# Attention with a soft mixture of experts on one core: all second layers as two column halves

## The chip, the core and the metric

The kernel runs on one core of one Trainium2 chip. The metric is the device time of one execution in microseconds, the median of several runs; lower is better. The engines are TensorE (PE, with its weight loads as PEld), VectorE (DVE), ScalarE (ACT), GpSimd (POOL) and SyncE (SP), which here issues all the DMAs.

## What is computed

First a causal attention with decay for 8 batches of 8 heads, 576 tokens and head size 64. Its result, reshaped to x of 4608 tokens by 512, goes through a soft mixture of 8 experts with 4 slots each:

```python
logits = x @ phi                                  # 4608 x 32
d = softmax of logits over the tokens             # how tokens make slots
slot_input = (d.T @ x).reshape(E, S_per_e, D)
for e in range(E):
    h = np.maximum(slot_input[e] @ w1[e], 0.0)    # 4 x 1024, "first layer"
    slot_out[e] = h @ w2[e]                       # 4 x 512,  "second layer"
c = softmax of logits over the slots              # how slots make tokens
return c @ slot_out.reshape(n_slots, D)           # 4608 x 512, float32
```

The output is 9.4 MB. The weights of the experts are 33.6 MB; the loads of the last 17 pieces of them are issued from 331.9 us on.

## The kernel before

The attention fills the first 324 us, head after head. The change touches only what comes behind it, the experts and the output; this part starts at about 331 us.

**Quarters.** The weights come in 64 pieces of 128 partitions by 1024 columns (512 KB), called quarters here. Eight belong to an expert: 0 to 3 are its first layer, 4 to 7 its second. `STEPS` (L34) is the order in which they are used, `ORDER` (L38) the order in which they are loaded; `weights(e, k)` finds one. 27 tiles hold the first ones, and when a step has used its quarters, `wstream` issues the next loads on SP into those tiles and into tiles of the attention that are free. SP issues in the order of the program.

**First layers.** `mlp1` makes the hidden values of an expert and `relu` gates them; `own` turns them so that `HT[e]` holds, for each of 8 chunks of 128 hidden units, a stationary matrix of 128x32.

**Second layers.** `mlp2(e, half, k)` multiplies one quarter with four matmuls of 256 columns each (in the trace each of them is two records, since float32 goes through TensorE in two passes). The stationary matrix has 32 columns, so four such matmuls write four different groups of 32 partitions of one PSUM bank. For experts below `DEFER` = 4, a quarter holds two chunks of hidden units over all 512 columns, and both halves of their steps add up in the bank `pv[0]`. For experts 4 to 7, a quarter holds four chunks over 256 columns, and columns 0 to 255 (half 0) add up in `po[0]`, columns 256 to 511 (half 1) in `po[1]`. The order is: experts 0 to 3 complete, half 0 of experts 4 to 7, half 1 of experts 4 to 7.

**From sums to output.** `so` takes the sum of experts 0 to 3 (ScalarE, L1002). When a half is complete, `gathered(n)` adds it (VectorE, L1012), `slots(n)` sums the four partition groups (TensorE, L1015), and `halve(n)` writes the result to `SO` as a rounded part (ScalarE, L1018) and the rest (VectorE, L1019). An output block is 128 tokens: `blocks(n0, n1, c)` multiplies the token weights with `SO`, 512 columns or one half of 256 (TensorE, L1032), copies each product out of PSUM, by turns on ScalarE and VectorE (L1033), into one of six staging tiles of 1024 columns, and issues a DMA for the call (SP, L1035). A half block of a token is a row of 1 KB in HBM, a full one 2 KB. A staging tile is used again when its DMA has landed.

**Token weights.** `cols(b)` turns the token weights of batch b for `blocks`, in four steps that `more(b, n)` takes: two transposes (L690), their cast (L694, ScalarE), three transposes, their casts (L694 and L696; VectorE for batches 2, 3, 5, 6, 7). Blocks of a batch can only go out behind its casts.

**The end.** While half 1 of experts 5 to 7 is multiplied, 10 half blocks of half 0 go out; three more stand between `gathered(1)` and `halve(1)`. Then follow half 1 of these 13 blocks and 23 full blocks. The order on every engine is the order of the program text.

Of the kernel before, what the change touches and what calls it, by code (L numbers as in the profile page):

```python
# [10 lines left out]
ALU = mybir.AluOpType  # L11
# [4 lines left out]
B, H, S, D = 8, 8, 576, 64  # L16
NE, SPE, DM, DF = 8, 4, 512, 1024
NS = NE * SPE
P = 128
# [9 lines left out]
NRES = 27  # L29
NQ = 8 * NE  # L30
QW = 1024
DEFER = 4

STEPS = tuple((e, 0) for e in range(8)) + tuple((e, k) for e in range(DEFER) for k in (4, 6)) + tuple((e, k) for k in (4, 6) for e in range(DEFER, 8))  # L34

SPLITS = {(6, 0): 4, (0, 6): 2, (1, 6): 3, (2, 6): 5, (3, 4): 6, (4, 4): 7}

ORDER = [8 * e + k + n for e, k in STEPS for n in range(2 if k else 4)]  # L38

# [29 lines left out]
def attn_softmoe(ctx: ExitStack, tc: tile.TileContext, qk, v, f, phi, w1, w2, cst, out):  # L69
    nc = tc.nc  # L70
# [51 lines left out]
    def wstream(*tiles):  # L122
        for t in tiles:
            axes = "abc"[: len(t.shape) - 1]
            t = t.rearrange(f"p {' '.join(axes)} -> p ({' '.join(axes)})")
            if len(quarter) < NQ:
                quarter.append(t[:, 0:QW])
                wload(len(quarter) - 1)

    def weights(e, k):  # L130
        return quarter[ORDER.index(8 * e + k)]
# [6 lines left out]
    pv = [psp.tile([P, 512], F32, name=f"pv{n}") for n in range(2)]  # L138
# [20 lines left out]
    def turn():  # L159
        ring.append(ring.pop(0))  # L160
        return ring[-1]
# [523 lines left out]
    def cols(b, bank):  # L685

        for ts in ((1, 2), (3, 4, 0)):
            pm = bank()
            for n, t in enumerate(ts):
                nc.tensor.transpose(pm[:, 128 * n : 128 * n + 128], CW[b][:, t].rearrange("p o r s -> p (o r s)").bitcast(F32), ident)  # L690
            yield
            at = S * b + 128 * (ts[0] - 1)
            copy = nc.vector.tensor_copy if b in (2, 3, 5, 6, 7) and 0 in ts else nc.scalar.copy
            copy(weights_of(at, 256).rearrange("p (u r c) -> p r u c", u=2, r=2), pm[:, 0:256].rearrange("p (r u c) -> p r u c", r=2, u=2))  # L694
            if 0 in ts:
                copy(weights_of(at + 256, 64), pm[:, 320:384])  # L696
            yield


    for g in range(1, NG):  # L700
        h0, h1 = 2 * g, 2 * g + 1
        u0, u1 = h0 + 3, h0 + 4
        b, w = divmod(g - 4, NPAIR)
# [154 lines left out]
    c = [cols(n, turn) for n in range(B)]  # L858
# [38 lines left out]
    po = [turn(), pv[0]]  # L897
    ring = [t for t in ring if t not in bank + po] + [st["lg", b]]
    HT = {}
# [8 lines left out]
    def mlp1(e, *ks):  # L908
        if e >= NE:
            return  # L910
        if 0 in ks:
            PH[e] = bank[e % 2]
        for k in ks:
            for j in range(4):
                nc.tensor.matmul(  # L915
                    PH[e][32 * j : 32 * j + 32, 0:256], slT[:, k, :], weights(e, k)[:, 256 * j : 256 * j + 256], start=(k == 0), stop=(k == 3)
                )

    def relu(e):

        scale = mk[:, e : e + 1]
        if e == 0:
            nc.vector.tensor_scalar(hs, PH[e][:, 0:256], scale, 0.0, op0=ALU.mult, op1=ALU.max)
        else:
            nc.vector.scalar_tensor_tensor(hs, in0=PH[e][:, 0:256], scalar=scale, in1=hs, op0=ALU.mult, op1=ALU.max)

    def blank_h(e):
        t = rest(e) if e < len(X) else quarter[NRES - 7 + e - len(X)][:, 640:896]
        HT[e] = t.rearrange("p (j c s) -> p j c s", j=4, c=2)
        nc.gpsimd.memset(HT[e], 0.0)  # L930

    def own():

        pm = turn()
        for c in range(2):
            nc.tensor.transpose(pm[:, 128 * c : 128 * c + 128], hs[:, 128 * c : 128 * c + 128], ident)
        for n in range(NE):
            mine = pm[:, 0:256].rearrange("p (c j s) -> p j c s", c=2, j=4)[:, :, :, 4 * n : 4 * n + 4]
            nc.vector.tensor_copy(HT[n][:, :, :, 4 * n : 4 * n + 4], mine)

    def mlp2(e, half, *ks):

        for k in ks or range(2):
            w = weights(e, 4 + 2 * half + k)
            for n in range(4 if e >= DEFER else 2):
                if e < DEFER:
                    fc, to = 4 * half + 2 * k + n, pv[0]
                    start, stop = e == half == 0, e == DEFER - 1 and half == 1
                else:
                    fc, to = 4 * k + n, po[half][:, 0:256]  # L950
                    start, stop = e == DEFER and k == 0, e == NE - 1 and k == 1
                m = to.shape[1]
                step = m if start or stop else 256
                for c in range(0, m, step):
                    nc.tensor.matmul(  # L955
                        to[32 * (fc % 4) : 32 * (fc % 4) + 32, c : c + step],
                        HT[e][:, fc // 2, fc % 2, :],
                        w[:, m * n + c : m * n + c + step],
                        start=start,
                        stop=stop,  # L960
                    )

    nc.vector.tensor_scalar_mul(mk, mk, fin[:, 2:3])
    for e in range(len(X)):
# [1 line left out]
    half = [slice(256 * n, 256 * n + 256) for n in range(2)]  # L966
    so = ctok.rearrange("p b t s -> p (b t s)")[:, 0:DM]
    used = 0
    for e, k in STEPS[:-4]:
        if k == 0:  # L970
            mlp1(e, 0, 1, 2, 3)
            relu(e)
        else:
            mlp2(e, k // 2 - 2)
        n = used + (2 if k else 4)
        wstream(*quarter[used : min(n, NRES)])
        used = n
        if (e, k) == (7, 0):
            next(c[4])
            next(c[4])  # L980
            own()
            next(c[4])
            next(c[4])
        if (e, k) == (1, 0):
            weigh(b)
            tokens(b, 0)
            combine(b, 0)
        if (e, k) == (3, 0):
            combine(b, 1)
            combine(b, 2)  # L990
        if (e, k) in SPLITS:
            split(SPLITS[e, k], 0, 1)
        if (e, k) == (6, 0):
            for n in range(len(X), NE):
                blank_h(n)
        if (e, k) == (0, 6):
            late.close()
            sp = ctx.enter_context(tc.tile_pool(name="sp", bufs=1))
            SO = sp.tile([P, DM], F32R, name="SO")
            last = [sp.tile([P, B // 2 * S - CUT[n]], F32R, name=f"cT{n}") for n in range(2)]  # L1000
        if (e, k) == (3, 6):
            nc.scalar.copy(so, pv[0])  # L1002

    pr = [t[:, 0:256] for t in bank]
    outv = out.rearrange("(n p) c -> p n c", p=P)
    NT = B * S // P
# [2 lines left out]

    def gathered(n):  # L1010

        nc.vector.tensor_tensor(so[:, half[n]], so[:, half[n]], po[n][:, 0:256], op=ALU.add)  # L1012

    def slots(n):
        nc.tensor.matmul(pr[n], srep, so[:, half[n]], start=True, stop=True)  # L1015
# [7 lines left out]
    def blocks(n0, n1, c=slice(0, DM)):  # L1023

        w = c.stop - c.start
        if state[1] + w * (n1 - n0) > QW:
            state[0:2] = state[0] + 1, 0
        o = stage[state[0] % len(stage)][:, state[1] : state[1] + w * (n1 - n0)]
        state[1] += w * (n1 - n0)
        for n in range(n0, n1):  # L1030
            pm = turn()[:, 0:w]
            nc.tensor.matmul(pm, weights_of(P * n, P), SO[:, c], start=True, stop=True)  # L1032
            copies[state[2] % 2](o[:, w * (n - n0) : w * (n - n0 + 1)], pm)  # L1033
            state[2] += 1
        nc.sync.dma_start(outv[:, n0:n1, c], o.rearrange("p (n c) -> p n c", c=w))  # L1035

    def more(b, n=2):

        for _ in range(n if b < B else 0):
            next(c[b])  # L1040

    gathered(0)
    mlp2(4, 1)
    slots(0)
    mlp2(5, 1)
    halve(0)
    ring += [po[0], bank[0]]
    blocks(0, 2, half[0])
    mlp2(6, 1)
    blocks(2, 4, half[0])  # L1050
    blocks(4, 6, half[0])
    mlp2(7, 1, 0)
    blocks(6, 8, half[0])
    blocks(8, 9, half[0])
    blocks(18, 19, half[0])
    mlp2(7, 1, 1)
    gathered(1)
    more(2, 1)
    blocks(19, 20, half[0])
    slots(1)  # L1060
    more(2, 1)
    blocks(20, 21, half[0])
    halve(1)
    blocks(21, 22, half[0])
    more(2, 1)
    ring += [po[1], bank[1]]
    then = {2: (2, 1), 4: (3, 2), 6: (3, 2), 18: (5, 2), 9: (5, 2), 13: (6, 2), 15: (6, 2), 22: (7, 2), 24: (7, 2)}
    for n0, n1 in ((0, 2), (2, 4), (4, 6), (6, 8), (8, 9), (18, 20), (20, 22)):
        blocks(n0, n1, half[1])
        more(*then.get(n0, (B,)))  # L1070
    for n0, n1 in ((9, 11), (11, 13), (13, 15), (15, 17), (17, 18)) + tuple((n, n + 2) for n in range(22, NT, 2)):
        blocks(n0, n1)
        more(*then.get(n0, (B,)))


# [39 lines left out]
```

## Time and profile before

| | us |
|---|---|
| median of 3 runs | 391.98 |
| lowest and highest run | 391.85 to 392.21 |
| span of the profiled execution, first to last instruction | 390.3 |
| TensorE busy in the span | 371.3 (95%) |
| VectorE busy | 280.4 (72%) |
| ScalarE busy | 259.6 (67%) |
| GpSimd busy | 252.5 (65%) |

Times inside the kernel are read from one profiled execution and count from its first instruction. The span lies 1.7 us below the median of the runs. Busy shares are means over stages that differ. The chain of waits follows the last instruction back to what released it. "DMA share" is the mean busy share of the core's 16 DMA engines in a stretch; when the queue is full it reads slightly over 1.

### The profile page before, as it was taken

Reading aid. Unit: us, or ns where it says so; the run is one execution under the profiler, and the core shown is the slowest. Engines: PE = TensorE matmul, PEld = TensorE weight load, DVE = VectorE, ACT = ScalarE, POOL = GpSimd, SP = SyncE. Lnnn points to the kernel's source line nnn. Section 1 sums busy time; section 2 is a strip of 40 time slices with the busy share of each in tenths; the row PEclk is TensorE's granted clock in tenths of the full one; section 3 lists DMA queues with packets and bytes.
Section 4 is the critical chain, followed back from the end, with each engine's and each line's share of the span. In section 5 each row is a group of like instructions: output and inputs, shape, how many; then the busy total and the mean of one; then the engine's idle time right before and its main releaser. Section 6 shows DMA issues by size and latency. Waiting matters only on the chain.

```text
span 390.3 us, 15100 instructions
## 1 busy us (share of the span) xinstructions
PE 371.3 (95%) x5867; PEld 333.4 (85%) x5867; DVE 280.4 (72%) x1074; ACT 259.6 (67%) x664; POOL 252.5 (65%) x349
## 2 busy tenths in 40 slices
PE   8989999999999999999999999999999998999860
PEld 8879999999999999999999999999999986567640
DVE  7968887878777978787878787878787635341670
ACT  8949776868686868677867786778776652021560
POOL 4977887878787878787878787878787841000000
PEclk9999999999999999999999999999999999999995
DMA  6874978676867787768677777777775889996798
GB/s 206 205 187 138 275 225 265 190 230 203 257 176 234 204 230 199 224 197 247 197 216 214 226 197 227 197 232 211 213 207 161 253 319 357 416 417 283 261 392 317
DMA packets 34343, 93.71 MB, mean 240 GB/s; under 512 B 4266, under 2 KB 8288, under 8 KB 34272
## 3 DMA queue, kind: packets, MB, share of 16 engines
q1 hardware_dynamic: 34272, 92.75, 76.4%
q8 instruction: 46, 0.75, 0.8%
q14 instruction: 25, 0.20, 0.1%
HBM read 63.93 MB, written 9.73 MB: 189 GB/s over the span
## 4 chain that ended last, share of the span: by engine, by line
PE 89%; DMA 5%; DVE 2%; ACT 1%; issue 1%; SPq 0%; ACTq 0%; DVEq 0%
PE pv L310 25%; PE ring L275 14%; PE s L222 12%; PE ring L276 12%; PE pv L337 4%; PE pv L955 4%; PE more L915 4%; PE lg L373 3%; PE ring L493 2%; DMA out<-RAW 2%; PE ds L457 2%; DMA V<-in_v 1%; PE pv L248 1%; DMA YA<-mr 1%; PE ring L1032 1%
## 5 line engine op out<-in xcount | busy, mean ns | idle before, releaser
L282 ACT ACTIVATE PTS<-ring 128x320 f32<-128x320 f32 (+2 forms) x256 | 119.5, 513 | 64.7 <-PE ring L276 39.7
L275 PE MATMUL ring<-YA,WA 67*128 67x320 f32 (+9 forms) x384 | 121.7, 330 | 0.1
L238 DVE CUSTOM_DVE_ANT_0 s<-s,mask 128x320 f32<-128x320 f32 (+3 forms) x256 | 109.1, 442 | 6.4 <-PE s L222 1.9
L276 PE MATMUL ring<-YB,WB 128*128 128x320 f32 (+4 forms) x384 | 110.6, 296 | 0.0
L310 PE MATMUL pv<-V,PTS 128*64 128x65 f32 x3200 | 104.5, 224 | 0.5 <-DMA V<-in_v 0.5
L310 PEld LDWEIGHTS pv<-V,PTS 128*64 128x64 f32 x3200 | 99.7, 138 | 3.3 <-issue 1.5
L222 PE MATMUL s<-WA,YA 66*128 66x288 f32 (+9 forms) x384 | 98.7, 313 | 0.9 <-ACT YA L180 0.8
L201 POOL TENSOR_TENSOR WB<-RAW,WB 64x576 fp32r<-64x576 f32 x64 | 90.5, 1414 | 12.4 <-DMA WB<-WA 7.2
L206 POOL TENSOR_TENSOR YB<-RAW,YA 64x576 fp32r<-64x576 f32 x64 | 89.7, 1419 | 2.5
L275 PEld LDWEIGHTS ring<-YA,WA 67*128 67x128 f32 (+3 forms) x384 | 69.9, 183 | 5.6 <-issue 2.1
L276 PEld LDWEIGHTS ring<-YB,WB 128*128 128x128 f32 (+1 forms) x384 | 70.1, 183 | 0.0
L222 PEld LDWEIGHTS s<-WA,YA 66*128 66x128 f32 (+1 forms) x384 | 63.1, 191 | 7.0 <-ACT PTS L282 1.3
L293 POOL TENSOR_SCALAR_AFFINE_SELECT PTS<-PTS 128x128 f32<-128x128 f32 (+1 forms) x128 | 31.3, 265 | 24.1 <-ACT PTS L282 22.2
L238 DVE DVE_READ_ACCUMULATOR2_ANT MT<- 128x1 f32 x310 | 44.0, 142 | 0.0
L290 POOL TENSOR_SCALAR_AFFINE_SELECT PTS<-PTS 128x384 f32<-128x384 f32 x64 | 33.3, 521 | 14.4 <-ACT PTS L282 10.4
L337 PE MATMUL pv<-cs,X 128*128 128x128 f32 x155 | 42.0, 277 | 0.0
L175 ACT CAST WA<-RAW 64x576 fp32r<-64x576 f32 x64 | 40.1, 669 | 1.2 <-DMA RAW<-in_qk 0.3
L180 ACT CAST YA<-RAW 64x576 fp32r<-64x576 f32 x63 | 39.5, 671 | 0.4
L238 DVE CUSTOM_DVE_ANT_0 s<-s,mask,MT 128x288 f32<-128x288 f32 x62 | 32.6, 526 | 9.0 <-PE s L222 0.2
L325 DVE TENSOR_SCALAR rl<-pv 128x5 f32<-128x5 f32 x64 | 10.5, 164 | 37.7 <-PE pv L310 37.1
L330 DVE TENSOR_TENSOR X<-pv,rl 128x320 f32<-128x320 f32 (+1 forms) x65 | 31.5, 486 | 2.4 <-DMA YA<-mr 0.3
L361 ACT COPY XTS<-pv 128x128 f32<-128x128 f32 (+1 forms) x124 | 28.6, 293 | 0.0
(214 smaller groups left out, 378.9 us busy)
## 6 DMA issues: line engine op xcount, KB each, us to landing
w<-in_w SPq DMA_DIRECT2D x45, 512.0 KB
RAW<-in_qk SPq DMA_DIRECT2D x31, 576.0 KB
V<-in_v SPq DMA_DIRECT2D x32, 325.0 KB
YB<-YA SPq DMA_DIRECT2D x30, 288.0 KB
WB<-WA SPq DMA_DIRECT2D x30, 288.0 KB
p<-in_w SPq DMA_DIRECT2D x6, 512.0 KB
out<-RAW SPq DMA_DIRECT2D x6, 512.0 KB
out<-p SPq DMA_DIRECT2D x5, 512.0 KB
```

The source lines that it names most:

```text
L175: nc.scalar.copy(WA[g % 3][0:64, S * h : S * h + S], RAW[g % 3][64:128, h])
L180: nc.scalar.copy(YA[g % 3][0:64, h, 64:640], RAW[g % 3][0:64, h])
L201: nc.gpsimd.tensor_tensor(t[0:64], RAW[g % 3][64:128, h], t[64:128].bitcast(F32), op=ALU.subtract)
L206: nc.gpsimd.tensor_tensor(YB[g % 2][64:128, h], RAW[g % 3][0:64, h], YA[g % 3][0:64, h, 64:640].bitcast(F32), op=ALU.subtract)
L222: nc.tensor.matmul(t[:, o : o + w], ya[0:m, h, 128 * blk : 128 * blk + 128], wa[0:m, j0 : j0 + w], start=True, stop=True)
L238: nc.vector.tensor_tensor_reduce(out=t[:, o : o + w], in0=t[:, o : o + w], in1=mask[:, m0 : m0 + w], scale=1.0, scalar=top if n == 3 else ...
L275: nc.tensor.matmul(o, wa[0:m, j0 : j0 + n], ya[0:m, h, 64 + i0 : 64 + i0 + w], start=True, stop=False)
L276: nc.tensor.matmul(o, wb[:, j0 : j0 + n], yb[:, h, i0 : i0 + w], start=False, stop=True)
L282: nc.scalar.activation(PT[i % 2][:, SEG_O[bank] : SEG_O[bank] + at], t[:, 0:at], AF.Exp, scale=0.125)
L290: nc.gpsimd.affine_select(d3, d3, pattern=[[0, 3], [1, 128]], compare_op=ALU.is_ge, fill=0.0, base=0, channel_multiplier=-1)
L310: nc.tensor.matmul(o[64 * u : 64 * u + 64, t, :], PT[i % 2][:, at : at + 64], V[:, g % 2, c, 65 * h : 65 * h + 65], start=(c == 0), stop=( ...
L337: nc.tensor.transpose(pm[:, 0:128], x[:, t, 128 * (p % 2) : 128 * (p % 2) + 128], ident)
```

## The change

All eight experts now use the 256-column layout that experts 4 to 7 had. The steps of the second layers become half 0 of experts 0 to 7, then half 1 of experts 0 to 7. `pv[0]` no longer holds a 512-wide sum, `so` takes no copy of it, and `gathered` becomes a copy. Host code lays the second-layer weights of experts 0 to 3 out like the others.

In the products of half 1, two quarters are followed by the slot sums of half 0, two more by the first two half blocks, and from there single quarters alternate with pairs of half blocks: 20 half blocks (10 pairs) stand between the products. Four more follow behind `halve(1)`. Transposes of token weights for batches 5, 2 and 3, which stood behind the products, now stand between them. Then come half 1 of the 24 blocks and 12 full blocks. So 48 half blocks and 12 full ones replace 26 and 23.

```diff
-DEFER = 4
-
-STEPS = tuple((e, 0) for e in range(8)) + tuple((e, k) for e in range(DEFER) for k in (4, 6)) + tuple((e, k) for k in (4, 6) for e in range(DEFER, 8))
-
-SPLITS = {(6, 0): 4, (0, 6): 2, (1, 6): 3, (2, 6): 5, (3, 4): 6, (4, 4): 7}
+STEPS = tuple((e, k) for k in (0, 4, 6) for e in range(8))
+
+SPLITS = {(6, 0): 4, (1, 4): 5, (2, 4): 2, (3, 4): 3, (4, 4): 6, (5, 4): 7}
...
-            for n in range(4 if e >= DEFER else 2):
...
+            for n in range(4):
+                nc.tensor.matmul(
+                    po[half][32 * n : 32 * n + 32, 0:256],
+                    HT[e][:, 2 * k + n // 2, n % 2, :],
+                    w[:, 256 * n : 256 * n + 256],
+                    start=e == k == 0,
+                    stop=e == NE - 1 and k == 1,
+                )
...
-    for e, k in STEPS[:-4]:
+    for e, k in STEPS[:-8]:
...
-        if (e, k) == (3, 6):
-            nc.scalar.copy(so, pv[0])
...
-        nc.vector.tensor_tensor(so[:, half[n]], so[:, half[n]], po[n][:, 0:256], op=ALU.add)
+        nc.vector.tensor_copy(so[:, half[n]], po[n][:, 0:256])
...
     gathered(0)
-    mlp2(4, 1)
+    mlp2(0, 1)
     slots(0)
-    mlp2(5, 1)
+    mlp2(1, 1)
     halve(0)
     ring += [po[0], bank[0]]
-    blocks(0, 2, half[0])
-    mlp2(6, 1)
-    blocks(2, 4, half[0])
-    blocks(4, 6, half[0])
-    mlp2(7, 1, 0)
-    blocks(6, 8, half[0])
-    blocks(8, 9, half[0])
-    blocks(18, 19, half[0])
-    mlp2(7, 1, 1)
+    early = [(0, 2), (2, 4), (4, 6), (6, 8), (18, 20), (20, 22), (22, 24), (24, 26), (8, 10), (10, 12)]
+    early_at = iter(early)
+    blocks(*next(early_at), half[0])
+    turns = {(3, 1): (5, 1), (4, 0): (5, 1), (4, 1): (5, 2), (5, 0): (2, 1), (5, 1): (2, 1), (6, 0): (2, 2), (7, 0): (3, 1)}
+    for e in range(2, NE):
+        for k in range(2):
+            mlp2(e, 1, k)
+            if (e, k) in turns:
+                more(*turns[e, k])
+            if (e, k) not in ((4, 1), (6, 0), (7, 1)):
+                blocks(*next(early_at), half[0])
     gathered(1)
-    more(2, 1)
-    blocks(19, 20, half[0])
+    more(3, 1)
     slots(1)
-    more(2, 1)
-    blocks(20, 21, half[0])
+    more(3, 2)
     halve(1)
-    blocks(21, 22, half[0])
-    more(2, 1)
+    early += [(12, 14), (14, 16)]
+    for n in early[-2:]:
+        blocks(*n, half[0])
     ring += [po[1], bank[1]]
-    then = {2: (2, 1), 4: (3, 2), 6: (3, 2), 18: (5, 2), 9: (5, 2), 13: (6, 2), 15: (6, 2), 22: (7, 2), 24: (7, 2)}
-    for n0, n1 in ((0, 2), (2, 4), (4, 6), (6, 8), (8, 9), (18, 20), (20, 22)):
+    then = {0: (6, 2), 4: (6, 2), 18: (7, 2), 22: (7, 2)}
+    for n0, n1 in early:
         blocks(n0, n1, half[1])
         more(*then.get(n0, (B,)))
-    for n0, n1 in ((9, 11), (11, 13), (13, 15), (15, 17), (17, 18)) + tuple((n, n + 2) for n in range(22, NT, 2)):
+    for n0, n1 in ((16, 18),) + tuple((n, n + 2) for n in range(26, NT, 2)):
         blocks(n0, n1)
-        more(*then.get(n0, (B,)))
...
-    w2 = np.concatenate([w2[:DEFER].transpose(0, 2, 1, 3, 4).reshape(DEFER, P, 8 * DM), w2[DEFER:].transpose(0, 2, 3, 1, 4).reshape(NE - DEFER, P, 8 * DM)])
+    w2 = w2.transpose(0, 2, 3, 1, 4).reshape(NE, P, 8 * DM)
```

The order on TensorE, at the end of the products of half 1 (in `L955 MATMUL pv_148<-w_121,w_132 32x256 x4`, the bank pv_148 takes the sums of half 1, w_121 is a quarter, w_132 holds an expert's `HT`). Before:

```order
L1015 MATMUL more_5693<-ctok,cs 128x256
L955 MATMUL pv_148<-w_123,w_133 32x256 x4
L955 MATMUL pv_148<-w_124,w_133 32x256 x4
L1032 MATMUL ring_152<-SO,cT 128x256
L1032 MATMUL ring_150<-SO,cT 128x256
L955 MATMUL pv_148<-w_125,w_134 32x256 x4
L955 MATMUL pv_148<-w_126,w_134 32x256 x4
L1032 MATMUL lg_5612<-SO,cT 128x256
L1032 MATMUL ring_151<-SO,cT 128x256
L1032 MATMUL pv_149<-SO,cT 128x256
L1032 MATMUL more_5693<-SO,cT 128x256
L955 MATMUL pv_148<-w_127,w_135 32x256 x4
```

After, from the same point behind half 0 (L1002 is the slot sum, L944 the product, L1019 the block):

```order
L1002 MATMUL more_5693<-ctok,cs 128x256
L944 MATMUL pv_148<-w_115,X_100 32x256 x4
L944 MATMUL pv_148<-w_116,X_100 32x256 x4
L1019 MATMUL ring_152<-SO,cT 128x256
L1019 MATMUL ring_150<-SO,cT 128x256
L944 MATMUL pv_148<-w_117,X_101 32x256 x4
L1019 MATMUL lg_5612<-SO,cT 128x256
L1019 MATMUL ring_151<-SO,cT 128x256
L944 MATMUL pv_148<-w_118,X_101 32x256 x4
L1019 MATMUL pv_149<-SO,cT 128x256
L1019 MATMUL more_5693<-SO,cT 128x256
L944 MATMUL pv_148<-w_119,X_5483 32x256 x4
```

The slot sum of half 0 moved ahead by eight quarters (w_115 follows it in place of w_123), and from w_117 on every quarter is followed by another kind of work.

The order on VectorE around the end of half 1 (L1012 gathers it, L1019 completes `SO`, L694 and L696 are casts of token weights, L1033 the copies of blocks). Before:

```order
L1033 COPY RAW_97<-ring_151 128x256
L1012 TENSOR_TENSOR ctok<-ctok,pv_148 128x256
L1033 COPY RAW_97<-ring_152 128x256
L1019 TENSOR_TENSOR SO<-more_5694,SO 64x256
L1033 COPY p_0_5327<-ring_151 128x256
```

After (L999 gathers, L1006 completes `SO`, L692 and L694 are the casts, L1020 the copies):

```order
L1020 COPY p_1_5328<-ring_152 128x256
L999 COPY ctok<-pv_148 128x256
L692 CAST cT_6017<-ring_150 128x2x2x64
L694 CAST cT_6017<-ring_150 128x64
L1006 TENSOR_TENSOR SO<-more_5694,SO 64x256
L1020 COPY p_0_5487<-ring_151 128x256
L1020 COPY p_0_5487<-more_5693 128x256
```

Two casts stand in the place of one copy ahead of the operation that completes `SO`, and the copies of the two fill pairs of half 0 stand behind it.

## Rows read from the trace of the kernel before

**Rows 1.** The page, chain that ended last: shares by engine.
```profile
PE 89%; DMA 5%; DVE 2%; ACT 1%; issue 1%; SPq 0%; ACTq 0%; DVEq 0%
```

**Rows 2.** Chain of waits from 300 us: start, duration, what.
```profile
347.11 11.49 PE pv L955 x192
...
372.73 8.62 DMA out<-RAW x2
```

**Rows 3.** Stretches of time: busy time by engine, granted clock, DMA share, GB/s.
```profile
348.00:357.00 9.00, 9.00 (x164) 7.42 (x163) 2.19 (x5) 1.98 (x5) 0.00 (x0) 1.00 1.02 416
357.00:358.00 1.00, 1.00 (x26) 0.93 (x21) 0.22 (x1) 0.00 (x0) 0.00 (x0) 1.00 0.76 299
358.00:361.00 3.00, 3.00 (x40) 1.42 (x36) 0.92 (x3) 0.74 (x2) 0.00 (x0) 1.00 0.07 30
361.00:362.00 1.00, 1.00 (x19) 0.53 (x8) 0.13 (x1) 0.00 (x0) 0.00 (x0) 1.00 0.08 16
362.00:364.00 2.00, 2.00 (x23) 0.98 (x22) 1.38 (x4) 1.29 (x4) 0.00 (x0) 1.00 0.46 157
364.00:367.00 3.00, 2.42 (x18) 1.85 (x15) 1.50 (x5) 1.29 (x4) 0.00 (x0) 1.00 1.09 379
367.00:369.00 2.00, 1.17 (x10) 0.96 (x10) 1.51 (x6) 1.04 (x4) 0.00 (x0) 1.00 0.71 238
369.00:373.00 4.00, 4.00 (x29) 3.47 (x27) 3.91 (x11) 3.76 (x10) 0.00 (x0) 1.00 1.03 345
373.00:388.00 15.00, 4.63 (x20) 2.65 (x18) 6.48 (x13) 4.94 (x10) 0.00 (x0) 0.72 1.05 399
388.00:390.30 2.30, 0.00 (x0) 0.00 (x0) 0.00 (x0) 0.00 (x0) 0.00 (x0) 0.50 0.17 65
```

**Rows 4.** TensorE in order of time: start, duration, line, operation, tiles, shapes, count.
```profile
354.03 4.57 PE L955 MATMUL pv<-w,w 128*32 128x256 f32 x80
358.53 0.70 PE L1015 MATMUL more<-ctok,cs 128*128 128x256 f32 x2
...
360.16 0.51 PE L1032 MATMUL ring<-SO,cT 128*128 128x256 f32 x2
360.60 1.07 PE L955 MATMUL pv<-w,w 128*32 128x256 f32 x16
...
362.26 0.64 PE L955 MATMUL pv<-w,w 128*32 128x256 f32 x8
362.83 0.51 PE L1032 MATMUL ring<-SO,cT 128*128 128x256 f32 x2
...
363.50 0.64 PE L955 MATMUL pv<-w,w 128*32 128x256 f32 x8
364.07 0.44 PE L690 MATMUL pv<-cs,w 128*128 128x128 f32 x2
...
364.69 0.70 PE L1015 MATMUL more<-ctok,cs 128*128 128x256 f32 x2
...
368.40 0.38 PE L690 MATMUL pv<-cs,w 128*128 128x128 f32 x2
...
368.86 0.49 PE L690 MATMUL pv<-cs,w 128*128 128x128 f32 x3
```

**Rows 5.** SyncE's queue: start, time and count of the output's first DMA issues.
```profile
361.23 5.19 SPq L1035 DMA_DIRECT2D out<-RAW  x8
```

**Rows 6.** VectorE in order of time, around the end of half 1.
```profile
360.71 0.42 DVE L1033 COPY RAW<-ring 128x256 f32<-128x256 f32 x1 [0.60 <-PE ring L1032]
...
364.21 0.42 DVE L1012 TENSOR_TENSOR ctok<-ctok,pv 128x256 f32<-128x256 f32 x1
...
366.00 0.43 DVE L1019 TENSOR_TENSOR SO<-more,SO 64x256 fp32r<-64x256 f32 x1
...
367.58 0.41 DVE L694 CAST cT<-lg 128x256 fp32r<-128x256 f32 x1
367.91 0.21 DVE L696 CAST cT<-lg 128x64 fp32r<-128x64 f32 x1
```

More of the change, by code (lines that the diff above doesn't have):

```diff
@@ L944, in mlp2 @@
             w = weights(e, 4 + 2 * half + k)
-            for n in range(4 if e >= DEFER else 2):
[L946 to L961, printed above, removed]
+            for n in range(4):
[6 more added lines that the diff above has]
+                )
     nc.vector.tensor_scalar_mul(mk, mk, fin[:, 2:3])
@@ L995, in attn_softmoe @@
                 blank_h(n)
-        if (e, k) == (0, 6):
+        if (e, k) == (1, 4):
             late.close()
```

## The prediction

> **What bounds the kernel now.** I read the shares of the chain of waits first. TensorE holds 89% of the chain and DMA 5% [rows 1], so a change in TensorE's order looks cheap or dear by TensorE's time alone. The end of the span says otherwise. The chain's last long piece is 8.62 us of output transfer, from 372.73 [rows 2], so I read the DMA share by stretches next [rows 3]. Four stages are to be seen there. Until 357 the queue is full with weights (share 1.02, 416 GB/s). About 357.8 the last weights land (0.76 of that one us) and the queue is all but empty until 362. From 362 to 369 it is fed in bursts (0.46, 1.09, 0.71). From 369 to 388.4 it is full without a break (1.03 and 1.05), while TensorE, VectorE and ScalarE fall idle. The reader should see two things: the end is set by when the output queue becomes full for good and by the bytes still due then, and before that point there is DMA time that nobody uses, some 6 us between 357.8 and 369 (1.93 MB went out there, 5.1 us of work at 379 GB/s, in 11.2 us). The change goes after that idle time. So the questions are how fast TensorE's new order feeds the queue, and when the queue is full for good.
>
> **First output earlier: 3.46 us.** The second layers are 32 blocks of weights ("quarters" of 1024 columns). The first output waits for 24 of them now (eight experts' share of half 0 and also half 1 of the first four experts) and for 16 after the change. The chain shows 347.11 as the start and the TensorE rows show 354.03 as the start of quarter 17 [rows 2, 4], so one quarter costs 6.92 / 16 = 0.43 us, and eight cost 3.46 us. The weights arrive in the same order of use and from the same issues, and every quarter is used at the old time or later, so no new wait on weights arises. What follows half 0 keeps its shape: gather on VectorE (a copy in place of an add, both 128x256; an add took 0.42 [rows 6], and the 0.42 us copies are as long, so zero), two quarters as cover, the slot sums, two quarters, first two blocks. The first output DMA, issued at 361.23 [rows 5], moves to 357.77, just when the weights end. The copy of the 512-wide sum on ScalarE that goes away lay beside products: zero.
>
> **The loop of products and blocks: this is where it costs.** Before, the tail of the products goes two quarters, two blocks, two quarters, four blocks, quarter, four blocks, quarter. After, twelve single quarters alternate with nine pairs of blocks and five groups of transposes. The products use the array as 128x32, the others as 128x128, and the TensorE rows show what an alternation costs [rows 4]: a lone quarter occupies 362.26 to 362.83 and 363.50 to 364.07, 0.57 us and not 0.43; a pair of blocks takes 360.16 to 360.60, 0.44, while four take 362.83 to 363.50, 0.67, so a block costs 0.12 and entering and leaving costs 0.2. One quarter plus one pair is 1.01 us, of which 0.67 is streaming and 0.34 is switching. Transposes inside a 128x128 stretch cost 0.11 each (two of them and two blocks take 368.40 to 368.86).
>
> The loop starts where the first pair of blocks ends, 360.60 - 3.46 = 357.14. Nine quarters with pairs: 9.09 us. Three of them also carry two transposes: 0.66. Two quarters with three transposes in place of blocks: 2 x (0.57 + 0.5) = 2.14. The last quarter: 0.57. Sum 12.4 us, so the products end at 369.5. They end at 364.07 now: half 1 is complete 5.4 us later than today. In the loop ScalarE and VectorE have one copy each per 1.01 us, of some 0.42 us [rows 6], and TensorE's buffers return six uses later, so TensorE alone sets this pace.
>
> The Trainium skill, "TensorEngine Tiling (Array Packing)", section "Key Properties", states that "Changing tiling mode (not just tile) drains the TensorE". That rule speaks against this order; the four transitions read above agree with it. Priced without it, the loop would be the first rival below.
>
> **The queue in the loop.** A pair of half blocks is 262,144 bytes, 0.69 us at the 379 GB/s of 364 to 367 and 0.76 us at the 345 GB/s of 369 to 373 [rows 3]; both stretches are almost all half blocks. I take 0.725. Ten pairs, 7.25 us of work, are spread from 358.4 to about 370.3. The queue is far from full, and it is idle 8.3 us in sum between 357.8 and the restart below, where it is idle some 6 us now.
>
> **The restart.** The last product and the slot sums stand 0.62 us apart (364.07 to 364.69), so slots start at 370.1. Then come three transposes, and on VectorE their two casts (0.41 and 0.21 [rows 6]) now stand ahead of the subtraction that completes half 1 (0.43), where one copy stands now. Transposes end near 371.2, casts 371.8, subtraction 372.2. The two fill pairs of half 0, meant to bridge this, have their VectorE copies behind that subtraction: first copy done 372.6, DMA issued 372.7. From issue to first traffic takes 0.7 us (361.23, and a share of 0.08 in the us from 361). So the queue is full for good from 373.4. VectorE then makes a pair each 0.42 us, with 1.2 us of casts in all, against 0.725 us of DMA per pair, so nothing starves it.
>
> **Bytes due.** After the restart: 14 pairs, 3.67 MB at 345 to 379 GB/s, 9.7 to 10.6 us, middle 10.15; six full pairs, 3.15 MB at the 399 GB/s of 373 to 388, 7.9 us. End of DMA 391.0 to 391.9, middle 391.5. It ends at 388.4 now (share 0.17 over 2.3 us [rows 3]). The difference is +3.1 us; of it some 2.3 are more idle time and 0.8 the 22 more half blocks in short rows. The profiled span is 390.3, 1.7 below the median of 391.98; what lies around it is unchanged. 391.98 + 3.0 = 395.0. The uncertain terms are the restart (0.7 either way: the loop's twelve iterations at 0.95 to 1.06, the casts) and the rate of the half blocks (0.5 either way): 393.6 to 396.2 for this case.
>
> The Trainium skill, "DMA: Bandwidth & Descriptors", section "Specifications", gives 512 B as the least transfer for line rate, by which rows of 1 KB would cost nothing extra; the trace differs (345 to 379 against 399 GB/s). By the page the 14 pairs would take 9.2 us and the sum would come to 394.1.
>
> **Rivals.** (a) Faster: the alternation costs only its streaming. Then 14 quarters at 0.43, 20 blocks at 0.12 and 12 transposes at 0.11 after the slots (358.53 + 0.6 - 3.46 = 355.7) end at 365.4, the restart is at 369.3, the DMA ends at 387.4 and the time is 391.98 - 1.0 = 391.0. It decides when a quarter with its pair takes under 0.75 us. For it: the order does feed the queue 3.5 us sooner. Against: every switch in the trace costs its 0.34. 10%. (b) No change: it needs a restart by 370.8 or so. Were the fill pairs on time (1 us) and the half blocks at 379 GB/s throughout (0.5), the time would be 393.5, still above; a loop shorter by a further 1 us must come on top, 392.5. 7%. (c) Slower still: half blocks crawl when the three engines copy and read beside them, as in 369 to 373, and the two copying engines fall behind in turn; at 10% under 345 GB/s the 14 pairs take 11.7 us: 396.6. 12%. That the change does not do what it says is excluded: the order on TensorE shows the 20 blocks between the products.
>
> **How the numbers follow.** My case has 71%. Range 392.4 to 396.4: it takes in the whole of my case and part of (b) and (c), and leaves (a) out. About 0.2% (0.8 us) is what a measurement of this kernel can tell from no change. Faster by more: 0.11 (case a and a little of b); same: 0.07; slower: 0.82.
>
> **What would show it.** First output DMA near 357.8. Between there and 369.5 single quarters of 0.57 us, and a DMA share of 0.5 to 0.65. Gather of half 1 near 369.6, against 364.21 now. A hole of 2 to 3 us in the DMA share between 370.5 and 373.4, then a full share to 391.5. I am wrong if the products end by 366, if the hole is missing, or if the queue is not full after the restart.

## The result and the profile after

The change takes 395.15 us (median; 394.83 to 396.43) against 391.98 for the kernel before, a ratio of 1.0081 with a 95% interval of 1.0062 to 1.0100: slower by 3.2 us, 0.8%. One execution of the kernel before took 398.23 us, a slow one, and stands in no comparison. The forecast was 395.0, range 392.4 to 396.4.

The profiled execution of the change is the one of 396.43 us, span 394.7. It lost 1.4 us far ahead of the change: the products of the second layers begin at 348.56 in place of 347.11 [rows 2]. TensorE's granted clock was 0.89 on average between 24 and 40 us, where the kernel before had 1.00; that this is what was lost is not shown (e8 below begins them at 348.30 and had 1.00 there). So in what follows times are compared from the first of these products on ("+22.3" is 22.3 us behind it). From there to the end of the span the kernel before takes 43.23 us, the change 46.13: +2.9.

TensorE in order of time, inside the loop and at its end (start, duration, line, operation, count; L944 is the product, L1019 the block, L1002 the slot sum):

```profile
358.54 0.64 PE L944 MATMUL pv<-w,X 128*32 128x256 f32 x8
359.11 0.39 PE L1019 MATMUL lg<-SO,cT 128*128 128x256 f32 x1
359.33 0.28 PE L1019 MATMUL ring<-SO,cT 128*128 128x256 f32 x1
359.54 0.64 PE L944 MATMUL pv<-w,X 128*32 128x256 f32 x8
...
370.16 0.64 PE L944 MATMUL pv<-w,w 128*32 128x256 f32 x8
371.35 0.70 PE L1002 MATMUL more<-ctok,cs 128*128 128x256 f32 x2 [0.55 <-DVE ctok L999]
```

A quarter occupies 358.54 to 359.11, 0.57 us, and with its pair 1.00 to the next quarter, as the rows of before gave it [rows 4]. The last quarter begins at +21.60 and takes its 0.57 us; the products of the kernel before ended 5.2 us sooner, at 364.07 [rows 4].

SyncE's issues (the first six of the output, and the next six; the columns are those of [rows 5]):

```profile
359.16 5.52 SPq L1022 DMA_DIRECT2D out<-RAW  x6
366.54 8.29 SPq L1022 DMA_DIRECT2D out<-p  x6
```

The first output goes out at +10.60, 3.5 us earlier than the +14.12 of before [rows 2, 5]. The earlier start is real and does not bring the end forward, as the stretches show (busy time of PE, PEld, DVE, ACT, POOL, then granted clock, DMA share, GB/s):

```profile
358.00:359.00 1.00, 1.00 (x14) 0.45 (x10) 0.40 (x2) 0.37 (x1) 0.00 (x0) 1.00 0.88 352
359.00:364.00 5.00, 5.00 (x56) 2.45 (x52) 1.94 (x6) 2.05 (x6) 0.00 (x0) 1.00 0.79 292
364.00:369.00 5.00, 5.00 (x56) 2.33 (x48) 2.21 (x7) 1.12 (x5) 0.00 (x0) 1.00 0.60 204
...
373.00:374.00 1.00, 0.79 (x6) 0.60 (x6) 0.97 (x3) 0.28 (x2) 0.00 (x0) 1.00 0.00 0
...
376.00:380.00 4.00, 3.93 (x25) 3.33 (x24) 3.74 (x12) 3.34 (x10) 0.00 (x0) 1.00 1.08 375
380.00:384.00 4.00, 1.31 (x5) 0.51 (x3) 2.07 (x3) 1.71 (x4) 0.00 (x0) 1.00 1.07 368
384.00:391.00 7.00, 0.00 (x0) 0.00 (x0) 1.38 (x2) 0.80 (x2) 0.00 (x0) 0.55 1.05 394
...
392.00:394.70 2.70, 0.00 (x0) 0.00 (x0) 0.00 (x0) 0.00 (x0) 0.00 (x0) 0.50 0.33 122
```

For 10 us the queue is fed at 292 and 204 GB/s (the last of the weights among it) while TensorE is busy all the time. Then it runs dry (0.00 in the us from 373), and it is full without a break from 374.8 on, until 392.9. In the kernel before the unbroken stretch begins at 368.3, inside the stretch 367 to 369 of [rows 3]. The kernel before, from 357.8, where all but a rest of its weights are in [rows 3], to that point, and from there to the end of the full queue:

```profile
357.81:368.32 10.51, 9.09 (x92) 5.25 (x85) 5.44 (x15) 3.98 (x12) 0.00 (x0) 1.00 0.50 176
368.32:388.41 20.09, 9.31 (x51) 6.80 (x51) 10.58 (x24) 9.10 (x20) 0.00 (x0) 0.78 1.04 385
```

The change, from the same distance to its first product:

```profile
359.26:374.82 15.56, 14.65 (x137) 7.97 (x138) 7.70 (x21) 6.12 (x19) 0.00 (x0) 1.00 0.55 192
374.82:392.86 18.04, 6.42 (x38) 5.02 (x36) 8.38 (x21) 6.94 (x18) 0.00 (x0) 0.77 1.05 378
```

Counted from the first product, the queue is full from +21.2 before and from +26.3 now, 5.1 us later; what is still due then takes 20.1 us before and 18.0 now, 2.1 less, since more half blocks are out. Together this is 3.0 us, where the two differ by 2.9 at the end.

VectorE around the end of half 1 (L999 gathers, L692 and L694 cast, L1006 completes SO, L1020 copies a block):

```profile
370.87 0.42 DVE L999 COPY ctok<-pv 128x256 f32<-128x256 f32 x1 [0.17 <-PE pv L944]
372.41 0.42 DVE L692 CAST cT<-ring 128x256 fp32r<-128x256 f32 x1 [1.12 <-PE ring L688]
372.75 0.21 DVE L694 CAST cT<-ring 128x64 fp32r<-128x64 f32 x1
373.00 0.43 DVE L1006 TENSOR_TENSOR SO<-more,SO 64x256 fp32r<-64x256 f32 x1
373.46 0.42 DVE L1020 COPY p<-ring 128x256 f32<-128x256 f32 x1
```

The casts stand ahead of the subtraction and the copies of the fill pairs behind it, so the fill pair's DMA goes out at +25.4, when most of the hole that it was to bridge (+23.8 to +26.2) is over.

### The profile page after: what moved, and what is told of

The parts are those of the page before. It is cut to its first block, busy times and chain, and to the rows that moved or that the text cites. A ratio compares the mean times of both kernels' runs of the same rounds, so it can differ in the third digit from the quotient of the medians.

```text
span 394.7 us, 15174 instructions
## 1 busy us (share of the span) xinstructions
PE 375.2 (95%) x5894; PEld 332.2 (84%) x5894; DVE 281.7 (71%) x1080; ACT 260.1 (66%) x668; POOL 253.1 (64%) x349
## 4 chain that ended last, share of the span: by engine, by line
PE 89%; DMA 4%; DVE 3%; ACT 1%; issue 1%; SPq 0%; DVEq 0%
PE pv L308 26%; PE ring L273 14%; PE ring L274 12%; PE s L220 12%; PE pv L335 4%; PE pv L944 4%; PE more L913 4%; PE lg L371 3%; DMA out<-p 2%; PE ds L455 2%; DMA V<-in_v 1%; PE pv L246 1%; PE ring L1019 1%; DVE s L236 1%; DMA PTS<-in_f 1%
```

## The experiments

My theory: entering and leaving the 128x32 products costs TensorE about 0.34 us each time; this and the blocks in the loop delay half 1; the end of the kernel is the point from which the queue stays full plus the bytes still due. The rivals: the loss is the bytes' own (more rows of 1 KB), or it comes from starting by halves whatever the loop looks like, or the early output does count and something else takes it back. Each result is given as a ratio to the kernel before, measured beside it; the change has 1.0081. Each ratio has an interval of 0.4 to 0.9 us either way, so between two of these kernels the times alone tell differences of about 1 us and more; the traces, counted from the first product, tell finer ones for one execution each. Every kernel starts from the change.

**Products of an expert together (e1_by_expert).** Six visits to the products in the loop in place of twelve, all else alike.

```diff
     for e in range(2, NE):
+        mlp2(e, 1)
         for k in range(2):
-            mlp2(e, 1, k)
             if (e, k) in turns:
                 more(*turns[e, k])
```

> The change with one thing altered: in the loop of half 1 the two quarters of an expert stand together and the blocks and transposes of both follow, so that products are left and entered 6 times in place of 12. Blocks, copies, transposes, bytes and DMAs are the same. My theory (leaving and entering the 128x32 products costs 0.34 us each time, this delays half 1, and the end is half 1's restart plus the bytes then due): 6 x 0.34 = 2.0 us less on TensorE, the products end 2 us earlier, the time falls by 1.7 to 2.1, from 395.1 to about 393.2. Rival 'short rows' (the 22 more half blocks in 1 KB rows make the loss): no change, 395.1. Rival 'streaming' (the blocks' own matmuls in the loop make the loss): no change either.

Measured: 393.52 us, ratio 1.0045 (1.0030 to 1.0059), 1.4 us less than the change. In the trace the last matmul of the products begins at +19.55 against +21.86, 2.3 us earlier, somewhat more than the 2.0 expected, with the same blocks in between. But the last pair of blocks now stands behind the last product, and its copy ahead of the gather on VectorE:

```profile
367.36 0.42 DVE L1020 COPY p<-ring 128x256 f32<-128x256 f32 x1 [0.97 <-PE ring L1019]
367.70 0.41 DVE L999 COPY ctok<-pv 128x256 f32<-128x256 f32 x1
```

So SO was complete only 1.4 us earlier, and the span's end came 1.4 us earlier. Short rows and streaming are the same in both kernels; neither can explain this.

**A switch by itself (e8_eight_small).** One small 128x128 matmul, whose result nobody reads, between the two quarters of each expert in half 0.

```diff
-            mlp2(e, k // 2 - 2)
+            mlp2(e, k // 2 - 2, 0)
+            nc.tensor.matmul(bank[0][:, 384:416], ident, srep[:, 0:32], start=True, stop=True)
+            mlp2(e, k // 2 - 2, 1)
```

> The price of a switch by itself: the change, with one small 128x128 matmul of 32 columns, whose result nobody reads, between the two quarters of each expert in half 0, where nothing stood. Eight products are left and entered more, with no copy, no DMA and some 0.03 us of streaming each. My theory: 8 x (0.34 + 0.03) = 3.0 us more before half 0 is complete, everything behind it moves by as much, and the time rises to about 397.9. Rival 'leaving the products costs only what is streamed': 0.2 to 0.4 us more, 395.3.

Measured: 398.70 us, ratio 1.0162 (1.0140 to 1.0185), 3.2 us more than the change. TensorE in half 0 of it (L964 is the small matmul; the last line is TensorE's load of its stationary matrix):

```profile
350.21 0.41 PE L964 MATMUL more<-cs 128*128 128x32 f32 x2
350.55 0.64 PE L944 MATMUL pv<-RAW,X 128*32 128x256 f32 x8
...
351.55 0.41 PE L964 MATMUL more<-cs 128*128 128x32 f32 x2
351.89 0.64 PE L944 MATMUL pv<-XTS,X 128*32 128x256 f32 x8
...
351.55 0.30 PEld L964 LDWEIGHTS more<-cs 128*128 128x128 f32 x2 [0.41 <-issue]
```

Two quarters and one small matmul take 1.34 us, where two quarters alone take 0.86: 0.48 for each, of which 32 columns are a small part. The gather of half 0 moved from +7.18 to +10.99, 3.81 us for eight, and the end of the span by the same 3.81 (by the ratios 2.0 to 4.3). Nothing else was added, so the price is that of leaving the products for one small matmul and entering them again. The size was under-estimated: I allowed 0.03 us for the small matmul, which is two records of its own in the trace (float32; how many passes a record stands for no run shows), and the loads of its stationary matrix alone lie for 0.30 us between the two quarters.

**Full blocks only (e4_no_halves), and the same with short rows (e9_short_rows).** No output between the products; all 36 blocks full, behind them. Then the same with each DMA issued as two column halves.

```diff
...
     for e in range(2, NE):
...
+        mlp2(e, 1)
     gathered(1)
-    more(3, 1)
+    more(5, 1)
     slots(1)
-    more(3, 2)
+    more(5, 1)
     halve(1)
...
+    for n0, n1 in [(n, n + 2) for n in (0, 2, 4, 6, 18, 20, 22, 24, 8, 10, 12, 14, 16, 26, 28, 30, 32, 34)]:
+        blocks(n0, n1)
+        more(*then.get(n0, (B,)))
```

```diff
-        nc.sync.dma_start(outv[:, n0:n1, c], o.rearrange("p (n c) -> p n c", c=w))
+        o = o.rearrange("p (n c) -> p n c", c=w)
+        for s in half:
+            nc.sync.dma_start(outv[:, n0:n1, s], o[:, :, s])
```

> The layout of the change with no output between the products: all 16 quarters of half 1 run on, then 36 full blocks go out in 2 KB rows. It takes away every switch in the loop, every short row and the early output together. My theory: products end at 361.6, SO is ready at 363.9, the queue is full from 366 on, 18 pairs of 1.31 us take 23.6, DMA ends at 389.6 against 388.4 before: time 393.1, so faster than the change by 2 us although its first output is 8 us later. Rival 'early output is what counts': it must be slower than the change, 397 or more (8 us of output time are not used).

> The price of short rows by itself: the kernel with no output between the products and 36 full blocks (393.92), with each DMA of two full blocks issued as two DMAs of one column half each. The same bytes, copies and matmuls, but all rows are 1 KB in place of 2 KB. My theory: all 9.44 MB go at 375 in place of 395 GB/s, 1.2 to 1.7 us more, about 395.3; the change has 22 of these 72 half blocks more than before, so short rows are 0.4 to 0.5 of its 3 us loss. Rival 'short rows make the loss': 22 of 72 must be worth 3 us, so 9 us more, 403. Rival 'short rows cost nothing at 512 B or more': no change.

Measured: 393.92 us, ratio 1.0051 (1.0033 to 1.0069), and 395.56 us, ratio 1.0087 (1.0067 to 1.0107). The first begins its output at +18.5, 8 us later than the change, and is 1.2 us faster than it, with an interval of 0.2 to 2.2 (0.8 us less gain than expected; 0.6 of it is that the queue was full from +19.5 on and not from 366, which is +18.9). So the early output is worth less than what comes with it, the loop and the short rows. Stretches with a full queue, of the first and then of the second kernel:

```profile
368.00:388.00 20.00, 9.80 (x36) 5.42 (x34) 10.57 (x21) 8.12 (x16) 0.00 (x0) 0.70 1.04 397
```

```profile
368.00:390.00 22.00, 9.33 (x37) 5.34 (x36) 10.86 (x21) 8.31 (x16) 0.00 (x0) 0.75 1.07 371
```

Rows of 1 KB go at 371 GB/s, rows of 2 KB at 397; for the whole output this is 1.4 us (0.0036 of 392), give or take 1. The kernel with short rows also has twice as many DMAs, so the price is that of both. The change has 22 of 72 half blocks more than before: 0.4 us of its 3, neither nothing nor the loss.

**Half 0 first with few breaks (e5_two_breaks, e7_one_break).** Half 0 early for 12 blocks only; 24 full blocks and all transposes stand behind the products. In the first kernel products are left three times; in the second once, with three pairs placed in the waits of gather, slot sums and subtraction.

```diff
+    early = [(0, 2), (2, 4), (4, 6), (6, 8), (18, 20), (20, 22)]
+    blocks(0, 2, half[0])
...
     for e in range(2, NE):
...
+        mlp2(e, 1)
+        for n in {3: early[1:3], 5: early[3:5]}.get(e, ()):
+            blocks(*n, half[0])
     gathered(1)
-    more(3, 1)
+    blocks(20, 22, half[0])
     slots(1)
-    more(3, 2)
     halve(1)
...
```

```diff
+    early = [(0, 2), (2, 4), (4, 6), (6, 8), (18, 20), (20, 22)]
+    for n in early[:3]:
+        blocks(*n, half[0])
...
     for e in range(2, NE):
...
+        mlp2(e, 1)
     gathered(1)
-    more(3, 1)
+    blocks(6, 8, half[0])
     slots(1)
-    more(3, 2)
+    blocks(18, 20, half[0])
     halve(1)
...
+    blocks(20, 22, half[0])
```

> The layout of the change with 12 half blocks of half 0 in place of 24, in two groups of four between groups of four quarters (products left and entered 3 times), one pair at the front and one pair ahead of the slot sums of half 1; 24 full blocks at the end and all transposes behind the products. My theory: products end at 357.1 + 3 x 1.86 + 2 x 0.67 = 364.1, restart at about 367.7, then 6 pairs of 0.725 and 12 of 1.31 us: DMA ends at 387.8, time 391.4 (391.0 to 392.0), at or a little below before. Rival 'the order by halves is at fault whatever the loop': 394 or more.

> The layout of the change with 12 half blocks of half 0, six of them in one group right behind SO's first half, then the twelve remaining quarters without a break, and three pairs in the waits of gather, slot sums and subtraction of half 1. Products are left once in place of three times (two breaks gave 392.15) and two blocks more stand behind the products. My theory: 2 x 0.34 + 0.24 = 0.9 us less ahead of half 1, the hole before the restart is filled by the three pairs, and the time falls by 0.7 to 1.0 against two breaks, to about 391.3, below before (391.8). Rival 'the end is set by the queue's total work': as two breaks, 392.1. Rival 'copies in the waits delay SO': 392.5 or more.

Measured: 392.15 us, ratio 1.0010 (0.9999 to 1.0021), and 391.43 us, ratio 0.9980 (0.9969 to 0.9990). So the order by halves is not at fault; with few breaks it is level with before, and with one it beats both kernels, by 0.8 us (0.4 to 1.2) and by some 4. The breaks are not the whole of these 4: there are 24 half blocks fewer than in the change, 0.5 us by the price of short rows above, and the pairs and transposes stand elsewhere. What breaks alone cost is told by e1 and e8. The first came 0.75 us above its forecast: the first pair of half 1 was issued at +20.2, so the queue was full from about +21 on and not from +20.6, and it then ran at 387 GB/s on the mean. TensorE in the second one:

```profile
357.20 1.93 PE L944 MATMUL pv<-w,X 128*32 128x256 f32 x32
358.96 3.64 PE L944 MATMUL pv<-w,w 128*32 128x256 f32 x64
362.52 0.50 PE L1019 MATMUL ring<-SO,cT 128*128 128x256 f32 x2
363.14 0.70 PE L1002 MATMUL more<-ctok,cs 128*128 128x256 f32 x2
```

Twelve quarters take 357.20 to 362.52, 5.3 us or 0.44 each, where the change's loop takes 12.2 with what stands in it (358.54 to 370.73).

**The passage to half 1 (e2_fill_first, e6_casts_behind).** A fill pair ahead of the slot sums, and batch 3's casts behind the subtraction; in the first kernel its three transposes go behind the first pair of half 1, in the second they stay behind the slot sums.

```diff
     more(3, 1)
+    blocks(12, 14, half[0])
     slots(1)
-    more(3, 2)
     halve(1)
...
+    blocks(0, 2, half[1])
+    more(3, 2)
+    blocks(14, 16, half[0])
```

```diff
     more(3, 1)
+    blocks(12, 14, half[0])
     slots(1)
-    more(3, 2)
+    more(3, 1)
     halve(1)
+    more(3, 1)
...
+    blocks(0, 2, half[1])
+    blocks(14, 16, half[0])
```

> The change with only the passage from half 0 to half 1 altered: the fill pair 12 to 14 stands ahead of the slot sums of half 1, and the three transposes of batch 3 with their two casts on VectorE stand behind the first pair of half 1 in place of ahead of the subtraction. The loop is unchanged. My theory: SO's second half is ready 0.6 us earlier, the hole in the DMA share that spans the 3 us ahead of the restart is filled with one pair (0.7 us), and the time falls by 1.0 to 1.4, to about 393.9. Rival 'bytes' (the queue's total work sets the end, not when it restarts): no change. Rival 'the hole is TensorE's' (products alone hold half 1): under 0.3.

> The second try at the passage alone. Like the kernel that put the fill pair 12 to 14 ahead of the slot sums, but the three transposes of batch 3 stay behind the slot sums (TensorE is not left idle there) and only their two casts on VectorE go behind the subtraction that completes half 1. My theory (the restart of the queue sets the end): SO is done 0.5 us earlier than in the change, one pair goes out in the hole, and if TensorE keeps its full clock the time falls by 0.8 to 1.2 us, to about 394.0. Rival 'what VectorE has to do up to the point where the queue stays full is the same in either order': SO earlier by 0.5, time within 0.4 us of the change.

Measured: 394.99 us, ratio 1.0072 (1.0048 to 1.0095), not to be told from the change, and 394.23 us, ratio 1.0054 (1.0035 to 1.0073), 1.1 us less than the change with an interval of 0 to 2.1. By their times the two cannot be told from each other (0.7 us, give or take 1.2), so what follows rests on one trace of each. The first missed its forecast although SO was complete 0.5 us earlier (+24.34 against +24.86) and the fill pair went out 2.2 us earlier. Its stretches show where the time went (columns as above):

```profile
371.00:372.00 1.00, 0.23 (x2) 0.00 (x0) 0.33 (x1) 0.37 (x1) 0.00 (x0) 1.00 0.77 260
...
373.00:374.00 1.00, 0.60 (x4) 0.49 (x4) 0.65 (x4) 0.37 (x1) 0.00 (x0) 0.89 0.00 0
374.00:375.00 1.00, 1.00 (x7) 1.00 (x7) 0.78 (x2) 0.59 (x2) 0.00 (x0) 0.50 0.78 262
375.00:376.00 1.00, 1.00 (x6) 1.00 (x5) 0.58 (x2) 0.42 (x2) 0.00 (x0) 0.50 0.70 248
```

TensorE waited 0.92 us for SO and 0.40 us for the casts, then had the lower clock level (1.2 of 2.4 GHz) for some 3.4 us, and the queue, which was to be full, got 262 and 248 GB/s, with gaps until +29.9. Whether the clock or the wait for the casts made these gaps is not separated. In the second kernel the transposes fill the first wait, TensorE keeps its clock, and the queue is full one us behind the hole:

```profile
371.00:372.00 1.00, 0.91 (x6) 0.87 (x7) 0.96 (x5) 0.49 (x2) 0.00 (x0) 1.00 0.58 195
372.00:373.00 1.00, 1.00 (x11) 1.00 (x10) 1.00 (x4) 1.00 (x4) 0.00 (x0) 1.00 0.00 1
373.00:374.00 1.00, 1.00 (x11) 0.98 (x10) 1.00 (x5) 0.96 (x5) 0.00 (x0) 1.00 0.99 327
```

SO's gain of 0.5 us is the same in both and is worth nothing in either: the queue starts again at +26.3, as in the change. In the second kernel the casts that left the way of the subtraction now stand ahead of the copies of the next pair. So far the rival named for the second kernel holds, that VectorE's work up to this point is the same in either order. What the second kernel gains in the trace, 0.7 us, is the fill pair that went out in the hole (0.26 MB less due behind it); the first lost it again in its gaps.

**All of them side by side**, from the profiled executions, counted from the first product of the second layers. "Last product" is the start of the last matmul of half 1, "SO complete" the end of the subtraction on VectorE; all columns but the last are us.

| kernel | last product begins | SO complete | span ends | between the last two | ratio to before |
|---|---|---|---|---|---|
| before | 16.65 | 19.32 | 43.23 | 23.91 | 1 |
| the change | 21.86 | 24.86 | 46.13 | 21.27 | 1.0081 |
| e1, six visits | 19.55 | 23.47 | 44.76 | 21.29 | 1.0045 |
| e6, casts behind | 21.85 | 24.35 | 45.43 | 21.08 | 1.0054 |
| e2, fill first | 21.85 | 24.34 | 46.36 | 22.02 | 1.0072 |
| e8, eight small | 25.66 | 28.67 | 49.94 | 21.27 | 1.0162 |
| e5, two breaks | 16.59 | 19.09 | 43.61 | 24.52 | 1.0010 |
| e7, one break | 15.45 | 18.34 | 42.95 | 24.61 | 0.9980 |
| e4, no halves | 14.41 | 16.90 | 44.94 | 28.04 | 1.0051 |
| e9, short rows | 14.41 | 16.90 | 46.70 | 29.80 | 1.0087 |

Where the same blocks are out before SO's second half (the change, e1, e8), the end follows SO by 21.3 us, wherever SO lies. Against before the change has 5.5 us more ahead of SO and 2.6 us less behind it: 2.9. The theory can be read directly from the stretches in which the queue is full, here of e1, e8 and e6 in this order:

```profile
371.65:389.68 18.03, 6.38 (x38) 5.01 (x36) 8.36 (x21) 6.92 (x18) 0.00 (x0) 0.79 1.05 378
378.37:396.40 18.03, 6.38 (x38) 5.01 (x36) 8.37 (x21) 6.93 (x18) 0.00 (x0) 0.77 1.05 378
373.00:390.29 17.29, 5.86 (x35) 4.71 (x33) 8.06 (x20) 6.67 (x17) 0.00 (x0) 0.74 1.05 379
```

The change, e1 and e8 are full from +26.3, +24.9 and +30.1 and all need 18.0 us from there; e6 is full from +26.3 like the change and needs 0.7 us less, its pair.

## Why the prediction was right

- **First output earlier by 3.46 us.** It was 3.5 (+10.60 against +14.12), through the same chain of gather, slot sums and subtraction.
- **One quarter with its pair at 1.01 us, the loop at 12.4.** The trace has 1.00 and 12.2: the gather of half 1 starts at +22.3, where the forecast's 369.6 is +22.5. TensorE was busy all through the loop (5.00 of 5 us twice), so nothing else paced it. The price of a switch, 0.34 us, was read from four transitions; e1 took six of them away and gained 2.3 us on TensorE, 0.38 each, and e8 added eight at 0.48 each, the small matmul included.
- **The queue in the loop.** The pairs came at the pace told and left the queue partly idle. The share that I named as a sign, 0.5 to 0.65 from the first output on to the end of the products, came out at 0.64 (359.25 to 370.95), 0.79 and 0.60 in its first and second 5 us. It entered no term of the sum.
- **The restart.** SO complete at 372.2 was the forecast, +25.1; it was +24.86. The hole between 370.5 and 373.4 was told as 2 to 3 us; the trace has 2.4, from +23.8 to +26.2. Of VectorE's order one half was right: the fill pairs' copies behind the subtraction left the hole unfilled, and e6 got the time of one pair back, 0.7 us. The casts ahead of the subtraction, which the working has in its path to 373.4, hold SO up by 0.5 us but not the queue: e6 moved them and the queue started at the same +26.3.
- **Bytes due.** The 14 pairs (3.67 MB) took 10.1 us, from +26.3 to +36.3, where the forecast had 10.15: 375 and 368 GB/s between 376 and 384, less in the first us. The six full pairs took 8.0, where it had 7.9. End of DMA: +44.4 was forecast, +44.3 measured.
- **Rival (a)**, switches without a price, fell with the 1.00 us of a quarter and its pair, and with e8. **Rival (b)** needed the queue full by 370.8, which is +23.7; it was full from +26.3. **Rival (c)**, half blocks at a crawl, needed 11.7 us for the 14 pairs that took 10.1.
- **The split of the loss.** The working gave 2.3 us to more idle time and 0.8 to short rows. By the stretches above the idle time between the weights' end and the full queue grew by 1.9 us (7.3 against 5.4; a full queue reads 1.04), and short rows are 0.4 by e9. Here the split was off though the sum was right. The remaining 0.6 us is about the time of the 0.2 MB more of weights that in this execution came in behind +10.7; no run was made for it.

What stays open is what the switch consists of. The Trainium skill, "TensorEngine Tiling (Array Packing)", section "Key Properties", states that a change of tiling mode drains TensorE. The 0.48 us for a matmul of 32 columns agrees with it, but no run here separates a drain from the loads of the new stationary matrices, which lie for 0.30 us in the same gap.

## What to carry to other kernels

When output is pulled ahead between the steps that still feed the other half of it, count what each insertion costs the engine that completes that half, its switches too, and not only the idle time that it fills elsewhere. Ask from which point the last resource stays full and what is still due there: idle time ahead of that point is only worth filling with pieces that delay it by less than they take off. Few, large groups of inserted work, and pieces that fit into waits that are there anyway, kept the early output and gave 0.8 us (e7) where twelve small insertions lost 3.2.

## What was not expected of the hardware

Gaps in TensorE's work did not cost the clock everywhere. In the kernel before TensorE was busy for 1.17 us of the two from 367 on and kept a granted clock of 1.00 [rows 3]. In e2 it was busy for 0.23 us of the one from 371 and for 0.60 of the one from 373, and then had 0.50 until about 377.2. While it had the lower level it was busy without a break (1.00 in the us from 374 and from 375), VectorE and ScalarE had idle time (0.58 and 0.42 in the us from 375), and the queue had gaps. That is one trace; the times do not tell this kernel from e6.
